# Retention attention on 64x64 quarter tiles of TensorE, and output written without transposes

## Chip, core and metric

The kernel runs on one core of a Trainium2 chip. The metric is the device time of one execution in microseconds (us). PE is the matrix engine TensorE, DVE, ACT and POOL are VectorE, ScalarE and GpSimdE, SP is the queue engine that issues all transfers here.

## What is computed

A decaying linear attention feeds two wide layers, all in float32 (the weights come as float64).

```python
B, H, S, D = 4, 8, 768, 64
gamma = 1.0 - 2.0 ** (-5.0 - np.arange(H))
for t in range(S):                       # state: B x H x D x D
    state = gamma * state + einsum('bhd,bhe->bhde', k[:, :, t], v[:, :, t])
    y[:, :, t] = einsum('bhd,bhde->bhe', q[:, :, t], state) / sqrt(D)
x = y.transpose(0, 2, 1, 3).reshape(3072, 512)
h = x @ w_in;  x = (h * cos(h)) @ w_out            # first layer, width 2048
h = x @ w_in2; x = elu(h) @ w_out2                 # second layer, width 2048
```

## The kernel before

The attention runs chunkwise. A unit is 128 tokens of one batch with all 8 heads; there are 24 units, four (one per batch) to a block of 512 tokens, six blocks. For unit n, chunk c = n // 4. `scores(n)` multiplies keys and queries (eight products, 64 deep, 128x128 out) and DVE masks the result into `pt`. `values(n)` adds, in PSUM, the state of the earlier chunks times the queries (for c > 0, eight products of 64x64 weights, 128 columns) and the values times `pt` (eight products, 128 deep, 64 wide, 128 columns). ACT and DVE split the sum into a high and a low part (`x_t`), the input of the first layer. `update(n)` multiplies keys and values of the unit into the state (eight products, 128 deep, 64x64). `state_unit(n)` makes the decayed state `aged(n)`; `scale_unit(n)` scales q and k.

The first layer's `hidden(blk, j)` takes block blk and the j-th of 8 pieces of the weights: 24 matmuls of 512 columns, then a chain of three ACT and two DVE passes out of PSUM. Attention of block blk + 1 stands between the `hidden` calls of block blk: `scores` before an even j, `values` after it, `update` after the next. During block 0 the weights are also decoded from float64 on ACT and DVE (`first_weights`), piece j being needed by `hidden(0, j)`.

Then come `project(0, ...)` (first layer out), `hidden2` and `project(1, ...)` (second layer). At the end each result tile `c`, which has features on the partitions and tokens along the free dimension, is turned by PE: `emit` makes two pieces of four 128x128 transposes each, with an ACT or DVE copy behind each piece, and writes rows of `out`; `last_half` does so for the two halves that are ready last. The list `turns` spreads these pieces between the matmul groups.

All instructions are recorded by `plan.op` with an engine, a supposed duration, and what they read and write. `Plan.deadlines` works out backward when each must begin. `Plan.run` then plays the program through on these durations and lets each engine take the ready instruction with the earliest deadline; PE keeps the recorded order. Operations of engine "ANY" go to DVE or POOL, whichever is free. Once the order is fixed, each engine's queue is strictly in order, SP's too. PSUM has three `eg` buffers of two banks (`hidden`, `scores`) and two `f` buffers of one bank (`values`, `update`, transposes).

Of the kernel before, what the change touches and what calls it, by code (L numbers as in the profile page):

```python
# [19 lines left out]
P = 128  # L20
# [4 lines left out]
TB = 512  # L25
# [6 lines left out]
WS = 4 * Q  # L32

# [41 lines left out]
class Plan:  # L75


    def __init__(self, slots):
        self.slots = slots
        self.ops = []  # L80
        self.queue = {tag: [] for tag in slots}

# [29 lines left out]
    def deadlines(self):  # L112
# [183 lines left out]
def retention_then_two_mlps(ctx: ExitStack, tc: tile.TileContext, attn, tab, weights, out):  # L296
# [22 lines left out]

    def dma(kb, out_, in_, r=(), w=(), lag=0):  # L320
        plan.op("SP", kb * PER_KB, lambda: nc.sync.dma_start(out=out_(), in_=in_()), r, w, lag)
# [120 lines left out]
    TAB, STATE, AGED, FALL = 0, 704, 1728, 2240  # L442
# [4 lines left out]
    def s_tab():  # L447
        return cst.t[:, 640:648].rearrange("p (h o) -> p h o", o=1)

    def g_tab():  # L450
        return cst.t[:, 648:652].rearrange("p (a o) -> p a o", o=1)
# [7 lines left out]

    def fall():  # L460
        return cst.t[:, FALL:FALL + H * P].rearrange("p (h t) -> p h t", h=H)
# [8 lines left out]
    fall_at = cst[FALL, FALL + H * P]  # L470
    unit, pt_t, x_t = {}, {}, {}
    tab_at = cst[TAB, TAB + 652]
# [8 lines left out]
    def scale_unit(n, lag=0):  # L481
# [5 lines left out]
        if n // B < UPB - 1:  # L487
            tt("ANY", (0.65, 1.25), k, k, lambda: s_tab().to_broadcast([P, H, D]), ALU.mult,
               [u[1536, 2048], tab_at], [u[1536, 2048]], lag=lag)
# [6 lines left out]

    def scores(n):
        u = unit[n]
        sc = Buf("eg", [P, 2, NPAIR, P])
        pt = Buf("w", [P, 2, NPAIR, P])  # L500
        pt_t[n] = pt

        def go():
# [8 lines left out]
        plan.op("PE", 1.0, go, [u[0, 1024]], [sc])  # L512
        flat = lambda x: (lambda: x.t.rearrange("p j a t -> p (j a) t"))
        tt("DVE", 1.23, flat(pt), flat(sc), fall, ALU.mult, [sc, fall_at], [pt], lag=-80)

    def values(n):
        c, b = divmod(n, B)
        u, pt = unit[n], pt_t.pop(n)


        xps = [Buf("f", [P, 2, P]) for _ in range(2)]

        def go():
            q = u.t[:, 0:512].rearrange("p (a t) -> p a t", a=NPAIR)
            for a in range(NPAIR if c > 0 else 0):
                for j in range(2):
                    r, o = slice(j * D, (j + 1) * D), j ^ (a % 2)
                    nc.tensor.matmul(  # L528
                        out=xps[a % 2].t[o * D:(o + 1) * D, a // 2, :], lhsT=aged(n)[r, a, :], rhs=q[r, a, :],
                        start=(a < 2), stop=False, skip_group_check=True,  # L530
                    )
            for a in range(NPAIR):
                for j in range(2):
                    h0, o = 1024 + (2 * a + j) * D, j ^ (a % 2)
                    nc.tensor.matmul(  # L535
                        out=xps[a % 2].t[o * D:(o + 1) * D, a // 2, :], lhsT=u.t[:, h0:h0 + D],
                        rhs=pt.t[:, j, a, :],
# [607 lines left out]
```

## Time and profile before

| what | us |
|---|---|
| median of three timed runs (1086.99 to 1088.24) | 1087.66 |
| profiled execution, first to last instruction (span) | 1086.3 |
| median less span: what lies around the span | 1.4 |
| PE busy in the span | 1063.6 |
| DVE busy | 807.5 |
| ACT busy | 659.9 |
| POOL busy | 229.1 |

Only the span of the profiled execution is recorded, not a time of its own beside it; the runs' median is set against it. An engine's busy time is the union of its instructions. Matmuls overlap in PE's pipeline, so a duration of one says little; the distance from one group's start to the next group's start is what it costs. A float32 matmul stands in the trace as two records. In the rows below, a timeline row has start, length, engine, line, what is written and read, tile and shape, and the number of records; brackets hold idle time before it and who ended it. A row of stretches has the stretch, its length, then each engine's busy time with its instructions, PE's granted clock (1.00 is 2.4 GHz), the share of the 16 transfer engines in use, and GB/s.

### The profile page before, as it was taken

Reading aid. Unit: us, or ns where it says so; the run is one execution under the profiler, and the core shown is the slowest. Engines: PE = TensorE matmul, PEld = TensorE weight load, DVE = VectorE, ACT = ScalarE, POOL = GpSimd, SP = SyncE. Lnnn points to the kernel's source line nnn. Section 1 sums busy time; section 2 is a strip of 40 time slices with the busy share of each in tenths; the row PEclk is TensorE's granted clock in tenths of the full one; section 3 lists DMA queues with packets and bytes.
Section 4 is the critical chain, followed back from the end, with each engine's and each line's share of the span. In section 5 each row is a group of like instructions: output and inputs, shape, how many; then the busy total and the mean of one; then the engine's idle time right before and its main releaser. Section 6 shows DMA issues by size and latency. Waiting matters only on the chain.

```text
span 1086.3 us, 15280 instructions
## 1 busy us (share of the span) xinstructions
PE 1063.6 (98%) x5704; PEld 856.5 (79%) x5704; DVE 807.5 (74%) x916; ACT 659.9 (61%) x805; POOL 229.1 (21%) x192
## 2 busy tenths in 40 slices
PE   7989999999999999999999999999999999999998
PEld 4767777778778888888887787777777888888886
DVE  6997787788789967657648898888889875565453
ACT  3876566655688753443445777877798744444442
POOL 3212550034114311000000453232223300010000
PEclk9999999999999999999999999999999999999999
DMA  9786999989999999999975558878868999999551
GB/s 345 298 281 215 338 325 324 329 277 350 328 323 336 317 326 335 337 342 329 348 293 195 221 229 303 311 293 323 314 232 280 361 349 298 385 326 326 200 204 59
DMA packets 115226, 323.32 MB, mean 298 GB/s; under 512 B 8656, under 2 KB 15440, under 8 KB 112592
## 3 DMA queue, kind: packets, MB, share of 16 engines
q1 hardware_dynamic: 115152, 322.35, 82.9%
q8 instruction: 45, 0.74, 0.3%
q14 instruction: 29, 0.24, 0.1%
HBM read 195.96 MB, written 126.35 MB: 297 GB/s over the span
## 4 chain that ended last, share of the span: by engine, by line
PE 84%; DVE 7%; ACT 4%; issue 2%; DMA 2%; POOL 0%; DVEq 0%; ACTq 0%; POOLq 0%
PE eg L907 41%; PE eg L607 23%; PE eg L680 11%; PE f L680 3%; ACT c L324 3%; PE eg L507 2%; PE f L535 2%; DVE c L329 2%; PE f L528 1%; DVE w L329 1%; DVE c L366 1%; PE f L808 1%; PE f L565 1%; DMA c<-in_weights 1%; ACT h L324 1%
## 5 line engine op out<-in xcount | busy, mean ns | idle before, releaser
L907 PE MATMUL eg<-hl,w 128*128 128x512 f32 x2016 | 464.2, 391 | 0.0
L907 PEld LDWEIGHTS eg<-hl,w 128*128 128x128 f32 x2016 | 376.7, 188 | 77.8 <-DVE h L837 0.3
L324 ACT ACTIVATE hl<-ld 128x1024 fp32r<-128x1024 f32 x168 | 177.5, 1060 | 232.8 <-PE eg L907 196.8
L329 DVE TENSOR_TENSOR hl<-ld,hl 128x1024 fp32r<-128x1024 f32 x168 | 209.8, 1260 | 106.5 <-ACT hl L324 106.3
L329 POOL TENSOR_TENSOR c<-c 128x512 f32<-128x512 f32 (+1 forms) x131 | 161.2, 1240 | 550.5 <-DVE c L329 126.7
L607 PE MATMUL eg<-hl,w 128*128 128x512 f32 x1152 | 274.8, 395 | 0.5 <-DVE w L329 0.5
L324 ACT ACTIVATE c<-c 128x1024 f32<-128x1024 f32 (+1 forms) x256 | 232.0, 919 | 40.7 <-DVE c L624 29.9
L607 PEld LDWEIGHTS eg<-hl,w 128*128 128x128 f32 x1152 | 213.9, 189 | 50.6 <-PE f L535 2.7
L324 ACT ACTIVATE c<-eg 128x1024 int32<-128x1024 f32 (+2 forms) x95 | 86.3, 908 | 73.2 <-PE eg L607 59.6
L329 DVE TENSOR_TENSOR c<-c 128x512 f32<-128x512 f32 (+2 forms) x137 | 91.5, 680 | 38.7 <-DMA c<-d 26.4
L680 PE MATMUL eg<-hl,w 128*128 128x512 f32 x432 | 111.3, 394 | 4.5 <-DVE c L329 1.9
L680 PEld LDWEIGHTS eg<-hl,w 128*128 128x128 f32 x432 | 79.9, 188 | 26.7 <-ACT h L324 3.8
L680 PE MATMUL eg<-ld,w 128*128 128x512 f32 x288 | 75.4, 399 | 2.2 <-ACT h L324 1.2
L629 DVE SCALAR_TENSOR_TENSOR c<-c,eg 128x1024 f32<-128x1024 f32 x48 | 58.4, 1218 | 19.5 <-ACT c L324 19.2
L624 DVE SCALAR_TENSOR_TENSOR c<-eg,c 128x1024 f32<-128x1024 f32 x48 | 58.6, 1221 | 13.9 <-ACT c L324 12.2
L680 PEld LDWEIGHTS eg<-ld,w 128*128 128x128 f32 x288 | 54.7, 192 | 16.4 <-ACT h L324 3.3
L329 POOL TENSOR_TENSOR ld<-ld,w 128x512 f32<-128x512 f32 x28 | 36.1, 1295 | 102.4 <-DMA ld<-in_attn 70.9
L423 DVE SCALAR_TENSOR_TENSOR w<-c,w 128x768 fp32r<-128x768 f32 (+1 forms) x48 | 56.7, 1196 | 1.3 <-ACT w L324 1.2
L366 DVE SCALAR_TENSOR_TENSOR c<-c,signs 128x512 uint32<-128x512 uint32 x64 | 51.2, 800 | 4.8 <-ACT signs L324 4.2
L324 ACT ACTIVATE signs<-c 128x512 f16<-128x512 f32 x64 | 50.1, 783 | 5.9 <-DVE c L366 4.7
L324 ACT ACTIVATE w<-c 128x1024 fp32r<-128x1024 f32 (+3 forms) x59 | 52.2, 916 | 0.3 <-PE eg L907 0.3
L324 ACT ACTIVATE h<-eg 128x512 f32<-128x512 f32 (+1 forms) x50 | 29.2, 584 | 34.8 <-PE eg L680 18.3
(62 smaller groups left out, 727.8 us busy)
## 6 DMA issues: line engine op xcount, KB each, us to landing
d<-c SPq DMA_DIRECT2D x205, 512.0 KB, 4.4
ld<-d SPq DMA_DIRECT2D x84, 1024.0 KB, 7.9
c<-d SPq DMA_DIRECT2D x93, 512.0 KB, 6.3
c<-in_weights SPq DMA_DIRECT2D x64, 512.0 KB, 6.1
ld<-in_attn SPq DMA_DIRECT2D x20, 1024.0 KB, 7.4
d<-h SPq DMA_DIRECT2D x32, 256.0 KB, 7.8
out<-c SPq DMA_DIRECT2D x11, 512.0 KB, 5.0
d<-c SPq DMA_DIRECT2D x16, 256.0 KB, 3.5
```

The costliest lines, as they stand in the source:

```text
L324: plan.op("ACT", us, lambda: nc.scalar.activation(out=out_(), in_=in_(), func=func, **kw), r, w, lag)
L329: return e.tensor_tensor(out=out_(), in0=a(), in1=b(), op=op)
L366: plan.op("DVE", 0.69, lambda: nc.vector.scalar_tensor_tensor(out=u(), in0=u(), scalar=3, in1=signs, op0=ALU.logical_shift_left, op1=ALU.b ...
L423: plan.op("DVE", 0.08 + 0.29 * (hi - lo), lambda: nc.vector.scalar_tensor_tensor(out=w.t[:, lo:hi, 1, :], in0=view(), scalar=turn, in1=hig ...
L507: nc.tensor.matmul(out=sc.t[:, j, a, :], lhsT=u.t[r, 512 + a * P:512 + (a + 1) * P], rhs=u.t[r, a * P:(a + 1) * P], start=True, stop=True,)
L528: nc.tensor.matmul(out=xps[a % 2].t[o * D:(o + 1) * D, a // 2, :], lhsT=aged(n)[r, a, :], rhs=q[r, a, :], start=(a < 2), stop=False, skip_ ...
L535: nc.tensor.matmul(out=xps[a % 2].t[o * D:(o + 1) * D, a // 2, :], lhsT=u.t[:, h0:h0 + D], rhs=pt.t[:, j, a, :], start=(c == 0 and a < 2), ...
L607: nc.tensor.matmul(out=h.t[:, half * TB:(half + 1) * TB], lhsT=quarter(j, qd, wpart, kc % 2), rhs=(xh, xl)[xpart].t[:, kc, :], start=(n == ...
L624: plan.op("DVE", 1.22, lambda: nc.vector.scalar_tensor_tensor(out=g.t, in0=h.t, scalar=1.0 / TWO_PI, in1=n(), op0=ALU.mult, op1=ALU.subtra ...
L629: plan.op("DVE", 1.22, lambda: nc.vector.scalar_tensor_tensor(out=g.t, in0=g.t, scalar=1.0, in1=h.t, op0=ALU.subtract, op1=ALU.mult,), [h, ...
L680: nc.tensor.matmul(out=out_(), lhsT=w.t[:, i, wpart, kc * P:(kc + 1) * P], rhs=x.t[:, xpart, kc, :], start=(start and n == 0), stop=(n == ...
L907: nc.tensor.matmul(out=acc.t[:, i * TB:(i + 1) * TB], lhsT=w[:, A_OF[p], wpart, i * P:(i + 1) * P], rhs=hl.t[:, gpart, k, :], start=(p in ...
```

## The change

Every product of the attention is cut into 64x64 tiles with 64 columns. A unit is now handled as two half chunks of 64 tokens.

- `scores(n)` holds the state products too (8 for each half chunk, into the same PSUM buffer) and 8 score products for each half chunk; for c = 0, 8 more between the halves. In the last chunk only the first half's state products are made. The mask pass covers 512 columns (768 for c = 0) where it covered 1024. `mid(n)`, the state between the halves, is a new DVE pass; for c = 0 DVE and not ACT stores the state. The keys of the last chunk are now scaled too.
- `carried(n)` (16 products with `aged` or `mid`) is a group of its own. A one-element POOL memset waits for it (`fence`), and `values(n)` (16 products, 24 for c = 0) waits for that memset.
- In blocks 1 to 4, `values(n)` and `scores(n + 1)` stand together before an even j, `carried(n + 1)` before the odd j. In block 0 they stand at tabulated places, some between the two halves of a `hidden`.
- The loads of the first four units and of weight pieces 0 and 1 get a fixed rank, so they go first and in that order.
- `emit` and `last_half` write `c` as it lies (4 KB or 2 KB a partition); transposes, their PSUM buffers and copies are gone, and the host permutes the result.

```diff
+        for n, rank in self.ranks.items():
+            start[n] = rank - 1e6
...
     def scores(n):
-        sc = Buf("eg", [P, 2, NPAIR, P])
-        pt = Buf("w", [P, 2, NPAIR, P])
+        c, batch = divmod(n, B)
+        blocks = [(ch, ch, ch * 2) for ch in range(2)] + ([(0, 1, 4)] if c == 0 else [])
+        wid = 2 * len(blocks) * HC
+        sc = Buf("eg", [P, 2, TB])
+        pt = Buf("w", [P, 2, wid])
+        sums = {0: (0, 0), 1: (0, 1)} if c else {0: (0, 0), 1: (0, 0)}
+        if c == UPB - 1:
+            del sums[1]
         def go():
-            for a in range(NPAIR):
-                for j in range(2):
-                    r = slice(j * D, (j + 1) * D)
-                    nc.tensor.matmul(
-                        out=sc.t[:, j, a, :], lhsT=u.t[r, 512 + a * P:512 + (a + 1) * P],
-                        rhs=u.t[r, a * P:(a + 1) * P], start=True, stop=True,
-                    )
-        tt("DVE", 1.23, flat(pt), flat(sc), fall, ALU.mult, [sc, fall_at], [pt], lag=-80)
+            for ch, (_, slot) in sums.items():
+                for a2 in range(2):
+                    for e in range(2):
+                        for j in range(2):
+                            h0, lo = at_head(j, ch, a2), wid + (slot * 2 + a2) * D
+                            r = slice(e * HC, (e + 1) * HC)
+                            nc.tensor.matmul(
+                                out=sc.t[j * D:(j + 1) * D, e, lo:lo + D],
+                                lhsT=u.t[r, 1536 + h0:1536 + h0 + D], rhs=u.t[r, 1024 + h0:1024 + h0 + D],
...
+            for cs, ct, at in blocks:
+                for a2 in range(2):
+                    for e in range(2):
+                        for j in range(2):
+                            r, h0 = slice(j * D, (j + 1) * D), (2 * a2 + e) * P
+                            ins = nc.tensor.matmul(
+                                out=sc.t[e * HC:(e + 1) * HC, j, (at + a2) * HC:(at + a2 + 1) * HC],
+                                lhsT=u.t[r, 512 + h0 + cs * HC:512 + h0 + cs * HC + HC],
+                                rhs=u.t[r, h0 + ct * HC:h0 + ct * HC + HC], start=True, stop=True,
...
+        plan.op("DVE", 0.42, lambda: after(nc.vector.tensor_tensor(
+            out=pair(mid(n)), in0=ds(0), in1=pair(aged(n)), op=ALU.add)), [sc, aged_at(n)], [mid_at(n)], -80)
...
+    def carried(n):
+            for ch, s in ((0, aged(n)), (1, mid(n))):
+                for a2 in range(2):
+                    for e in range(2):
+                        for j in range(2):
+                            r, o = slice(j * D, (j + 1) * D), j ^ e
+                            ins = nc.tensor.matmul(
+                                out=xps[e].t[o * D:(o + 1) * D, a2, ch * HC:(ch + 1) * HC], lhsT=s[r, e * 2 + a2, :],
+                                rhs=q[r, 2 * a2 + e, ch * HC:(ch + 1) * HC],
...
+        def fence():
+            ins = nc.gpsimd.memset(fences[0:1, n:n + 1], 0.0)
+            wait(ins, xps_t[n])
...
+        plan.op("POOL", 0.1, fence, xps, [fence_b[n]], -60)
...
+                            if n in xps_t:
+                                wait(ins, xps_t.pop(n))
...
-    def update(n):
...
-    def emit(sb, name, c, half, blk):
+    def emit(c, half, blk):
+        dma(4, lambda: out[blk, half], lambda: c.t, [c])
...
-                        nc.tensor.transpose(ps.t[:, k, :], c.t[:, lo + k * P:lo + k * P + P], ident)
+        dma(2, lambda: out[2 * sb, 1][:, i * TB:(i + 1) * TB], lambda: c.t, [c])
...
+    for k, n in ((0, 4), (3, 5), (7, 6), (11, 7), (14, 8)):
+        slots_of.setdefault((0, k), []).append((scores_of, n))
+    for k, n in ((2, 4), (6, 5), (10, 6), (13, 7), (15, 8)):
+        slots_of.setdefault((0, k), []).append((carried_of, n))
+    for k, n in ((3, 4), (7, 5), (11, 6), (14, 7)):
+        slots_of.setdefault((0, k), []).insert(0, (values_of, n))
+    for blk in range(1, NBLK - 1):
+        for i in range(B):
+            n = (blk + 1) * B + i
+            slots_of[blk, 4 * i] = [(values_of, n), (scores_of, n + 1)]
+            slots_of[blk, 4 * i + 2] = [(carried_of, n + 1)]
...
-    while turns:
-        turns.pop(0)()
```

On PE, in the middle of block 1, one unit's period stood so before (L607 is `hidden`, L565 `update`, L507 `scores`, L528 and L535 the two parts of `values`; a number behind x counts matmuls):

```order
L607 MATMUL eg<-hl,w 128x512 x24
L565 MATMUL f<-ld 64x64 x8
L507 MATMUL eg<-ld 128x128 x8
L607 MATMUL eg<-hl,w 128x512 x24
L528 MATMUL f<-ld,w 64x128 x8
L535 MATMUL f<-w,ld 64x128 x8
```

Of the change (L679 `hidden`, L598 `carried`, L629 `values`, L536 and L547 the state and score products of `scores`):

```order
L679 MATMUL eg<-hl,w 128x512 x24
L598 MATMUL f<-ld,w 64x64 x16
L679 MATMUL eg<-hl,w 128x512 x24
L629 MATMUL f<-w,ld 64x64 x16
L536 MATMUL eg<-ld 64x64 x16
L547 MATMUL eg<-ld 64x64 x16
```

There are still two breaks in the `hidden` stream per unit; 32 products became 64 smaller ones, and three groups of one tile size now adjoin.

On DVE, just before the first `hidden` of block 0, the rows before were these (`hl<-hl,w` scales unit 3, `hl<-f` makes the low part of the layer's input, `w<-c,w` the low part of weight piece 0, `w<-eg,w` is a mask):

```order
L329 TENSOR_TENSOR hl<-hl,w 128x512
L329 TENSOR_TENSOR hl<-f,hl 128x2x128
L329 TENSOR_TENSOR w<-c,w 128x4x256
L329 TENSOR_TENSOR hl<-f,hl 128x2x128
L329 TENSOR_TENSOR w<-eg,w 128x1024
```

Of the change (L563 is the mask, L572 the stored state, L374 a step of decoding weights, `ld<-ld,w` scales a unit):

```order
L563 TENSOR_TENSOR w<-eg,w 128x768
L572 COPY w<-eg 128x256
L374 SCALAR_TENSOR_TENSOR c<-c,signs 128x512
L337 TENSOR_TENSOR hl<-f,hl 128x2x128 x2
L337 TENSOR_TENSOR ld<-ld,w 128x512
L337 TENSOR_TENSOR w<-c,w 128x4x256
L337 TENSOR_TENSOR hl<-f,hl 128x2x128 x2
```

The last of these low parts, which the first `hidden` reads, had 24 DVE instructions ahead of it and has 33 now: two more scalings (fewer fall to POOL), four state copies, a copy for the mask table, a decoding step and a decayed state.

On SP, the first loads stood so before (`in_attn` are the units, `in_tab` tables, `in_weights` the float64 weights):

```order
L321 DMA ld<-in_attn 128x1024
L321 DMA w<-in_tab 128x652
L321 DMA ld<-in_attn 128x1024
L321 DMA ld<-in_attn 128x512 x2
L321 DMA ld<-in_attn 128x1024
L321 DMA ld<-in_attn 128x512 x2
L321 DMA c<-in_weights 128x1024
L321 DMA ld<-in_attn 128x512
L321 DMA c<-in_weights 128x1024
L321 DMA hl<-in_attn 128x1024
L321 DMA ld<-in_attn 128x512
L321 DMA ld<-in_attn 128x2048
```

Of the change:

```order
L327 DMA ld<-in_attn 128x1024
L327 DMA w<-in_tab 128x588
L327 DMA ld<-in_attn 128x512 x2
L327 DMA ld<-in_attn 128x1024
L327 DMA ld<-in_attn 128x512 x2
L327 DMA ld<-in_attn 128x1024
L327 DMA ld<-in_attn 128x512 x2
L327 DMA c<-in_weights 128x1024 x2
L327 DMA hl<-in_attn 128x1024
L327 DMA hl<-in_attn 128x512 x2
L327 DMA c<-in_weights 128x1024 x2
L327 DMA ld<-in_attn 128x2048
```

Each unit now comes whole before the next, and unit 4 (the last row of each) comes behind weight pieces 0 and 1.

## Rows read from the trace of the kernel before

**Rows 1.** The page's head and PE's busy time, share and instructions.
```profile
span 1086.3 us, 15280 instructions
PE 1063.6 (98%) x5704; PEld 856.5 (79%) x5704; DVE 807.5 (74%) x916; ACT 659.9 (61%) x805; POOL 229.1 (21%) x192
```

**Rows 2.** Stretches: opening, block 0, blocks 1 to 4, block 5, `project(1)`.
```profile
core 0: us, PE busy (x) PEld busy (x) DVE busy (x) ACT busy (x) POOL busy (x), PEclk, DMA share, GB/s
0.00:27.15 27.15, 21.13 (x232) 13.19 (x232) 17.76 (x25) 10.31 (x21) 8.95 (x11) 1.00 0.93 344
27.15:91.34 64.19, 61.06 (x450) 47.82 (x448) 58.60 (x74) 50.44 (x72) 14.74 (x13) 0.97 0.76 279
91.34:322.52 231.18, 231.18 (x1714) 183.43 (x1713) 185.51 (x231) 147.21 (x186) 67.36 (x58) 1.00 0.89 316
322.52:366.04 43.52, 43.52 (x193) 36.05 (x192) 39.60 (x44) 37.37 (x42) 15.67 (x20) 1.00 0.94 333
...
840.10:1086.30 246.20, 241.30 (x1105) 198.25 (x1103) 144.36 (x139) 110.66 (x118) 16.17 (x10) 1.00 0.80 280
```

**Rows 3.** Timeline of PE, one unit's period between blocks 1 and 3.
```profile
163.03 0.69 PE L565 MATMUL f<-ld 128*64 128x64 f32 x16
163.65 1.16 PE L507 MATMUL eg<-ld 64*128 64x128 f32 x16
164.74 5.76 PE L607 MATMUL eg<-hl,w 128*128 128x512 f32 x24
170.43 0.67 PE L528 MATMUL f<-ld,w 64*64 64x128 f32 x16
171.03 1.09 PE L535 MATMUL f<-w,ld 128*64 128x128 f32 x16
172.05 5.74 PE L607 MATMUL eg<-hl,w 128*128 128x512 f32 x24
177.72 0.69 PE L565 MATMUL f<-ld 128*64 128x64 f32 x16
```

**Rows 4.** Timeline of PE matmuls begun before 47.63 us.
```profile
47.61 0.34 PE L528 MATMUL f<-ld,w 64*64 64x128 f32 x4
```

**Rows 5.** Timeline of PE weight loads begun before 47.69 us.
```profile
47.61 0.21 PEld L528 LDWEIGHTS f<-ld,w 64*64 64x64 f32 x8 [0.35 <-issue]
```

**Rows 6.** Stretches of block 0, DVE busy alone, then clock and transfers.
```profile
27.15:42.00 14.85, 14.33 (x17) 1.00 0.90 352
42.00:57.00 15.00, 14.66 (x19) 1.00 0.72 253
57.00:72.00 15.00, 14.53 (x20) 0.89 0.77 268
```

**Rows 7.** Timeline of PE around its longest wait in block 0.
```profile
65.75 0.98 PE L528 MATMUL f<-ld,w 64*64 64x128 f32 x16 [2.61 <-DVE hl L329]
```

**Rows 8.** Groups of DVE and POOL in blocks 1 to 4, shapes apart.
```profile
L329 DVE TENSOR_TENSOR w<-eg,w 128x1024 f32<-128x1024 f32 x16 | 19.5, 1217 | 3.3 <-PE eg L507 3.1
L329 DVE TENSOR_TENSOR c<-c 128x512 f32<-128x512 f32 x27 | 18.7, 692 | 0.7 <-POOL c L329 0.2
L329 DVE TENSOR_TENSOR w<-f,w 128x256 f32<-128x256 f32 x12 | 5.0, 421 | 12.4 <-PE f L565 12.4
L329 POOL TENSOR_TENSOR c<-c 128x256 f32<-128x256 f32 x3 | 2.2, 740 | 24.1 <-DMA d<-c 20.8 <-DVE c L329 2.3 <-DVE c L366 1.1
```

**Rows 9.** Timeline of PE, `project(1)` up to its first transposes.
```profile
840.08 46.41 PE L907 MATMUL eg<-hl,w 128*128 128x512 f32 x204
886.33 0.60 PE L808 MATMUL f<-ident,c 128*128 128x128 f32 x4
```

**Rows 10.** Timeline of all engines, the end.
```profile
1080.68 0.39 PE L907 MATMUL eg<-hl,w 128*128 128x512 f32 x1
1081.52 0.42 DVE L837 COPY h<-eg 128x256 f32<-128x256 f32 x1 [2.74 <-ACT h L324]
1082.97 0.37 SPq L321 DMA_DIRECT2D out<-h  x1
```

More of the change, by code (lines that the diff above doesn't have):

```diff
@@ new lines, in go, with after, mask @@
+            last.append(ins)
+            return ins
+        plan.op("PE", 1.05 if c else 1.2, go, [u], [sc])
+        def after(ins):
+            wait(ins, last[0])
+            return ins
+        def mask():
+            return after(nc.vector.tensor_tensor(
+                out=pt.t.rearrange("p j (h t) -> p j h t", t=HC),
+                in0=sc.t[:, :, 0:wid].rearrange("p j (h t) -> p j h t", t=HC),
+                in1=fall()[:, :, 0:wid // HC, :], op=ALU.mult))
+        plan.op("DVE", 0.68 if c else 0.95, mask, [sc, fall_at], [pt], -80)
@@ new lines, in scores, with go @@
+        if c < UPB - 1:
+            plan.op("DVE", 0.42, lambda: after(nc.vector.tensor_tensor(
+                out=pair(state(batch)), in0=ds(1), in1=pair(mid(n)), op=ALU.add)),
+                [sc, mid_at(n)], [state_at(batch)], -40)
+    xps_of, xps_t, fence_b = {}, {}, {}
+    fences = keep.tile([1, NU], F32, name="fences")
+    def carried(n):
+        u = unit[n]
+        xps = [Buf("f", [P, 2, P]) for _ in range(2)]
+        xps_of[n] = xps
+        def go():
+            q = u.t[:, 0:512].rearrange("p (a t) -> p a t", a=NPAIR)
+            for ch, s in ((0, aged(n)), (1, mid(n))):
[6 more added lines that the diff above has]
+                                rhs=q[r, 2 * a2 + e, ch * HC:(ch + 1) * HC],
+                                start=(ch == 0 and a2 == 0), stop=False, skip_group_check=True,
+                            )
+            xps_t[n] = ins
+        plan.op("PE", 0.6, go, [u[0, 512], mid_at(n), aged_at(n)], xps)
+        fence_b[n] = Buf(None, [1, 1])
+        fence_b[n].t = fences
+        def fence():
+            ins = nc.gpsimd.memset(fences[0:1, n:n + 1], 0.0)
+            wait(ins, xps_t[n])
+            xps_t[n] = ins
+            return ins
+        plan.op("POOL", 0.1, fence, xps, [fence_b[n]], -60)
@@ L516, in values @@
     def values(n):
         c, b = divmod(n, B)
-        u, pt = unit[n], pt_t.pop(n)
-        xps = [Buf("f", [P, 2, P]) for _ in range(2)]
+        u, pt = unit.pop(n), pt_t.pop(n)
+        xps = xps_of.pop(n) if c else [Buf("f", [P, 2, P]) for _ in range(2)]
+        blocks = [(ch, ch, ch * 2) for ch in range(2)] + ([(0, 1, 4)] if c == 0 else [])
         def go():
[L524 to L537, printed above, removed]
-                        start=(c == 0 and a < 2), stop=(a >= NPAIR - 2), skip_group_check=True,
-                    )
@@ L543, in values @@
+        plan.op("PE", 0.6 if c else 0.8, go, [u[1024, 1536], pt] + ([fence_b[n]] if c else []), xps)
         if b == 0:
@@ L617, in hidden @@
             plan.op("PE", 12 * MM, go, [xh, xl] + need, [h[half * TB, half * TB + TB]])
+            if half == 0:
+                for step, n in between:
+                    step(n)
         u = Buf("c", [P, 2 * TB])
```

256 lines of the change are left out of this document (111 added, 145 removed).

## Prediction

> **What bounds the kernel now.** I began with the page's head: PE is busy for 98% of a span of 1086.3 us [rows 1]. A share alone does not say that work taken from PE shortens the run, so I split the span at stage boundaries [rows 2]. In blocks 1 to 4 PE is busy for all of 231.18 us, in block 5 for all of 43.52 us. There PE's own work is the time, and the other engines have room (DVE 185.51 of 231.18). Block 0 is different: 64.19 us, of which PE works 61.06, with a granted clock of 0.97. Then I looked at one unit's period on PE [rows 3], at how quickly products on different tiles start [rows 4, 5], at DVE in block 0 [rows 6, 7], at single costs on DVE and POOL [rows 8], and at the end of the program [rows 9, 10].
>
> Block 5 holds no attention, so it gives the price of `hidden` alone: 43.52 us for 192 matmuls, 0.2267 each, 5.44 for the 24 of one call [rows 2]. Four blocks of that are 174.1, so attention costs blocks 1 to 4 the other 57.1 us. [Rows 3] split this by the distance between starts: `update` 163.03 to 163.65, 0.62; `scores` to 164.74, 1.09; the state part of `values` 170.43 to 171.03, 0.60; its other part to 172.05, 1.02; together 3.33 us a unit. A `hidden` between them takes 5.69 and 5.67 where it takes 5.44 undisturbed, so each break in its stream costs 0.24 more.
>
> **Attention on quarter tiles.** First the price of the new groups. `update` is 8 passes of 64 columns on two tiles at a time, 0.62; `scores` is 8 passes of 128 columns on two tiles, 1.09 [rows 3]. The difference, 0.47, is what 8 times 64 columns cost, so a pass of 64 columns is 0.059 us, and 0.15 of a group is its beginning and end. The open question is whether four 64x64 tiles run together at this pace. The nearest row is the state part of `values`, which uses 64x64 tiles: its 16 records of 128 columns take 0.60, the 16 records on two half-wide tiles behind it take 1.02 [rows 3]. Four of its matmuls begin within 0.03 us [rows 4], and eight weight loads begin within 0.09 us, so that loads do not queue for each other beyond one round [rows 5]. I take four abreast. Bounds for a group of 16 new products (8 passes of four tiles): 0.62 if all four run together as the two do in `update`, 1.09 if two at a time (16 passes of 0.059 and 0.15).
>
> So `carried` costs 0.62. `values` and `scores` together are 24 passes: 1.56 as one run (0.15 and 24 times 0.059), 1.71 if the beginning and end are paid twice. The rows show no boundary between two groups of the same tile size, so both ends stay; I take 1.60, nearer to one run, because within a group the next tile follows without a gap. (The Trainium skill, TensorEngine Tiling (Array Packing), Key Properties, says that a change of tiling mode drains TensorE and a change of tile alone does not. By it the boundary would be free, 1.56; [rows 3] show only boundaries with a change of mode, so they neither support nor deny it.)
>
> A unit then costs 2.22 where it cost 3.33, with the same two breaks. In the last chunk the pair has 20 passes, 1.32 to 1.47, I take 1.36. From the first `hidden` of block 1 to the end of block 4, PE did 12 `update`, 15 `scores` and 16 `values`: 7.4, 16.4 and 25.9, in all 49.7 us. Of the change it does 11 full pairs (17.6), 4 short ones (5.4), 15 `carried` (9.3) and one lone `values` (0.6): 32.9. Breaks are 31 in both. **Saved: 16.8 us** (14.7 with every boundary paid, 17.4 with none). One `carried` and one set of state products have moved into block 0.
>
> What else must keep up there? DVE's mask falls from 1.22 us to about 0.69, while `mid` adds 0.42 [rows 8], so DVE has no more work than before, 185.5 us in 214. The PSUM of a `hidden` is reused two calls later: the time in between falls from about 9 us to 8 us, against 5.4 us for which it is left alone in block 5's stream twice over (10.9). Transfers are the tighter side: 0.89 of the engines over 231 us becomes 0.96 over 214, and the highest share that the rows show without a PE wait is 0.94 [rows 2]. I put **1 us back** for that, 0 to 5.
>
> **Opening and block 0.** DVE is busy for 43.5 of the first 44.9 us of block 0 [rows 6], and PE's longest wait there, 2.61 us, ends with DVE [rows 7]. Saving PE's time in this stretch mostly makes PE wait longer. DVE's work is about equal: four masks less half, four `mid` more. Before the first `hidden` it grows: two scalings and a decoding step at 0.69, four state copies and a decayed state at 0.42, less four shorter masks (0.27 each, estimated between the rows for 512 and 1024 columns) and a mask table that is 0.1 cheaper; 2.1 + 2.1 - 1.1 - 0.1, near 3 us. Against it stand 9.4 us in which DVE is idle in the opening (17.76 busy of 27.15 [rows 2]); loads in the order of need should fill some of this. I let the first `hidden` come 1.5 us later (1 earlier to 3 later). After 72 us DVE has room (the other 15.1 of its 58.6 us in 19.3 [rows 2, 6]), and the last `hidden` calls of block 0 stand with cheaper groups: about 2.5 us back, with part of the wait's consequences. **Net 1 us less** until block 1, from 4 less to 4 more.
>
> The fixed order of the loads alone moves no bytes: the units were first before too, and it is the tables that DVE waits for, whose place is unchanged. I cost it at nothing beyond the above; it is hidden behind DVE, and if DVE were faster it would be worth less than the 1.5 us.
>
> The fence puts POOL between `carried` and `values`. The wait is covered by a `hidden` of 5.44 us; POOL is busy for 67 of 231 us [rows 2]. Cost: nothing, unless a POOL instruction ahead of the memset itself waits (below).
>
> **Output.** From its first matmul at 840.08 to the last at 1080.68 plus 0.23, `project(1)` takes 240.8 us on PE [rows 9, 10]. Its 1008 matmuls at 0.2267 (204 of them take 46.25 [rows 9]) are 228.5. The rest, 12.3, is transposes, the breaks beside them and the waits of the last halves. All of it goes: **12.3 us**. The copies behind the transposes are not on the path. At the end, the halves are copied by 1081.94, then turned and copied again, and the last transfer is issued at 1082.97 [rows 10]; now it can be issued at 1082.0: **0.95 us**. Its own time I leave as it is.
>
> **Sum.** Of the span of 1086.3: -1.0 - 16.8 + 1.0 - 12.3 - 0.95 = -30.05, so 1056.2; with the 1.4 us that lie around it, 1057.6 us. The median stands to the span as before (1087.66 to 1086.3).
>
> **Rivals.**
> *Two tiles at a time.* If 64x64 tiles with 64 columns run in pairs, a pass of four costs 0.117 us. Then a pair of groups costs 2.96 and `carried` 1.09, 4.05 a unit where it was 3.33. Blocks 1 to 4: 60 in place of 49.7, 10.3 more; block 0 and the opening 4 to 5 more by the same price; output 13.3 less: 1088 to 1091, not faster, and slower from about 0.11 us a pass on. Against it: [rows 4], four starts within 0.03 us, though with 128 columns. Chance 0.05.
>
> *A floor for each matmul.* If starts kept a distance of 0.025 us whatever the tile, four would need 0.10 us, hidden in today's passes of 128 columns but not in those of 64. Pairs 2.55, short pairs 2.15, `carried` 0.95: 52 in place of 49.7; with the output about 1077. Against it: [rows 4] again, whose four starts would fill 0.075 us and not 0.03. Chance 0.03. (The Trainium skill, TensorE: Matmul & The Clock Gate, Part 1, gives about 25 ns as the least distance of starts however small the matmul; by that rule this rival would win. The trace disagrees for matmuls on different tiles, by the 0.03 us.)
>
> *Someone else becomes the bound in blocks 1 to 4.* Transfers, at a share of 0.89 already, or a fence late behind a POOL instruction that waits for its own transfer: one such wait was 20.8 us [rows 8], and a `values` would wait for what exceeds 5.4 us. Before, PE waited for neither there. If half of the 16.8 is lost, 1066; if all, 1074. Chance 0.13.
>
> *Less than forecast*, if the opening improves too and boundaries are free: under 1052, chance 0.04.
>
> **The numbers.** The forecast has 0.75, with its own range of 1052 to 1063. Its bounds add up to: -4, -17.4, 0, -12.3, -1, which gives 1053, and +4, -14.7, +5, -12, -0.9, which gives 1069. The range 1052 to 1067 leaves out the first two rivals, the worse half of the third and the last. Faster by over 0.2% (what a measurement of this kernel can just tell from no change, 2 us) holds for all but the first rival: 0.94; same 0.02; slower 0.04.
>
> **What would show it.** `carried` near 0.62 from start to start, `values` and `scores` together near 1.6, an unbroken `project(1)` of 228.5 us, blocks 1 to 4 near 215 with PE busy throughout, first `hidden` between 26 and 30 us. Passes of 0.1 us and more, PE waits on POOL or on transfers in blocks 1 to 4, or a block 0 over 68 us would prove me wrong.

## The result, and the profile after

The changed kernel takes **1059.6 us** (median of four runs, 1058.5 to 1060.6), the kernel before in runs beside it 1088.0: ratio 0.973, 95% interval 0.971 to 0.975. The profiled execution took 1058.54, its span is 1056.8, where [rows 1] had 1086.3. The forecast was 1057.6, its span 1056.2. The total is close; its parts are not all. The median lies 2.0 above the forecast: 0.6 in the span, 0.3 because 1.7 us and not 1.4 lie around it, and 1.1 because the execution that was profiled was the fastest of the four. For the same reason the spans differ by 29.5 where the medians differ by 28.3.

The page of the changed kernel, head, PE's busy row and the queues that bring instructions:

```profile
span 1056.8 us, 18290 instructions
PE 1028.8 (97%) x7204; PEld 832.6 (79%) x7208; DVE 806.6 (76%) x931; ACT 651.5 (62%) x788; POOL 230.8 (22%) x213
...
q8 instruction: 56, 0.92, 0.4%
q14 instruction: 29, 0.24, 0.1%
```

PE has 34.8 us less to do than in [rows 1] and is idle for 28.0 us where it was idle for 22.7. So about 5 us of PE's saving came back as waiting. The stretches say where (opening, block 0, blocks 1 to 4, `hidden2`, `project(1)` to the end; to be held against [rows 2]):

```profile
core 0: us, PE busy (x) PEld busy (x) DVE busy (x) ACT busy (x) POOL busy (x), PEclk, DMA share, GB/s
0.00:30.98 30.98, 20.31 (x596) 13.19 (x600) 18.98 (x32) 10.67 (x20) 6.53 (x9) 0.93 0.93 339
30.98:95.67 64.69, 61.09 (x836) 46.89 (x832) 59.33 (x82) 49.10 (x69) 14.93 (x19) 0.95 0.74 267
95.67:308.16 212.49, 212.02 (x2568) 170.83 (x2561) 180.56 (x250) 141.69 (x180) 61.32 (x63) 1.00 0.93 331
...
580.16:822.51 242.35, 234.09 (x1009) 187.52 (x1008) 211.20 (x259) 195.35 (x264) 89.22 (x73) 1.00 0.79 284
822.51:1056.80 234.29, 229.28 (x1009) 188.85 (x1007) 137.20 (x128) 103.97 (x104) 12.51 (x9) 1.00 0.82 289
```

One correction makes the first three comparable. The new group of `values` and `scores` that ends block 0 does 1.5 us of work (94.12 to 95.67) where before `update` and `scores` stood, and block 0 also holds a `carried` more. (The prediction says "from the first `hidden` of block 1", but its count of 11 full pairs includes this one; from 95.67 on there are 10. So its sum has to be held against the time from 94.12.) Measured from the point at which that group begins, 94.12, opening and block 0 together are 2.8 us longer than the 91.34 of before, and blocks 1 to 4 take 214.04 (to 308.16), 17.1 less than 231.18. `hidden2` took 245.55 before (below) and is 3.2 shorter, `project(1)` to its last matmul 10.7 shorter (240.6 to 229.9), and from there to the end it is 1.2 shorter. Block 5 and `project(0)` are unchanged to 0.1. The sum: +2.8 - 17.1 - 3.2 - 10.7 - 1.2 = -29.4, the difference of the spans within rounding.

The timeline of PE in the middle of block 1 shows the price of a unit; it answers to [rows 3]:

```profile
155.96 0.69 PE L598 MATMUL f<-ld,w 64*64 64x64 f32 x32
156.58 5.74 PE L679 MATMUL eg<-hl,w 128*128 128x512 f32 x24
162.25 0.69 PE L629 MATMUL f<-w,ld 64*64 64x64 f32 x32
162.76 0.65 PE L536 MATMUL eg<-ld 64*64 64x64 f32 x32
163.23 0.65 PE L547 MATMUL eg<-ld 64*64 64x64 f32 x32
163.81 2.56 PE L679 MATMUL eg<-hl,w 128*128 128x512 f32 x10
```

`carried` costs 0.62 (155.96 to 156.58), `values` with `scores` 1.56 (162.25 to 163.81), in all 2.18 where it was 3.33. The three groups follow each other at 0.51 and 0.47, and the middle one's 0.47 is just eight passes of 0.059: the joint between groups of one tile size is free.

The opening is where the forecast failed. PE there, from the `values` of the second unit to the first `hidden` (L679; L629 is `values`, L536 and L547 `scores`, L996 filler matmuls):

```profile
17.49 0.80 PE L629 MATMUL f<-w,ld 64*64 64x64 f32 x39
21.77 0.35 PE L629 MATMUL f<-w,ld 64*64 64x64 f32 x9 [3.47 <-issue]
21.94 0.68 PE L536 MATMUL eg<-hl 64*64 64x64 f32 x32
22.41 0.91 PE L547 MATMUL eg<-hl 64*64 64x64 f32 x48
23.25 0.82 PE L996 MATMUL eg<-c 128*128 128x512 bf16 x2
24.00 0.79 PE L629 MATMUL f<-w,ld 64*64 64x64 f32 x35
26.09 0.45 PE L629 MATMUL f<-w,ld 64*64 64x64 f32 x13 [1.29 <-issue]
27.93 1.24 PE L629 MATMUL f<-w,hl 64*64 64x64 f32 x48 [1.38 <-DVE hl L337]
29.55 0.69 PE L536 MATMUL eg<-ld 64*64 64x64 f32 x32 [0.38 <-DVE ld L337]
30.07 0.99 PE L547 MATMUL eg<-ld 64*64 64x64 f32 x32
30.98 0.79 PE L679 MATMUL eg<-hl,w 128*128 128x512 f32 x1
```

Twice PE stops in the middle of a group of 48 records, after 39 and after 35, with nothing that it waits for ("issue"), for 3.47 and 1.29 us. Nothing differs there in the operands. A third such stop, of 0.48 us, cuts the first `hidden` itself: its first record begins at 30.98, the second at 32.10 after a wait of 0.33 for DVE, and only from 33.80 on does it run unbroken. From 30.19 to 37.01 PE's granted clock is 0.50, that is 1.2 GHz, after waits of 1.29, 1.38 and 0.38 us, and from 9.71 to 13.12 too, after one of 1.98; in the opening of the kernel before it stays at 1.00 [rows 2]. So this `hidden` gives way to the next group only at 40.30, 9.3 us after its first record; in the kernel before that took 5.7 (27.15 to 32.82). And DVE in the stretch of the first stop:

```profile
18.44 0.69 DVE L337 TENSOR_TENSOR hl<-hl,w 128x512 f32<-128x512 f32 x1
22.57 0.76 DVE L337 TENSOR_TENSOR hl<-f,hl 128x256 fp32r<-128x256 f32 x2 [3.44 <-ACT hl L332]
```

DVE's next row in its queue is the low part of the very `values` group in which PE stopped, so DVE stands idle for 3.44 us too. Before, DVE had no gap of over 0.2 us between 17.2 and 28.5 us.

### The profile page after: what moved, and what is told of

Same layout as the page of the kernel before. It is cut to its first block, busy times and chain, and to the rows that moved or that the text cites. A ratio compares the mean times of both kernels' runs of the same rounds, so it can differ in the third digit from the quotient of the medians.

```text
span 1056.8 us, 18290 instructions
## 1 busy us (share of the span) xinstructions
PE 1028.8 (97%) x7204; PEld 832.6 (79%) x7208; DVE 806.6 (76%) x931; ACT 651.5 (62%) x788; POOL 230.8 (22%) x213
## 5 line engine op out<-in xcount | busy, mean ns | idle before, releaser
L679 PE MATMUL eg<-hl,w 128*128 128x512 f32 x1152 | 277.0, 397 | 3.0 <-DVE c L704 1.5
L337 POOL TENSOR_TENSOR c<-c 128x512 f32<-128x512 f32 (+1 forms) x141 | 173.3, 1240 | 479.5 <-DVE c L337 170.4
L679 PEld LDWEIGHTS eg<-hl,w 128*128 128x128 f32 x1152 | 214.2, 189 | 51.5 <-DVE w L337 1.9
L699 DVE SCALAR_TENSOR_TENSOR c<-eg,c 128x1024 f32<-128x1024 f32 x48 | 58.6, 1220 | 19.2 <-ACT c L332 17.1
L377 DVE SCALAR_TENSOR_TENSOR c<-c 128x512 uint32<-128x512 uint32 x64 | 52.6, 831 | 0.7
L374 DVE SCALAR_TENSOR_TENSOR c<-c,signs 128x512 uint32<-128x512 uint32 x64 | 50.2, 785 | 0.8 <-ACT signs L332 0.5
L332 ACT ACTIVATE h<-eg 128x512 f32<-128x512 f32 (+1 forms) x50 | 29.2, 584 | 29.1 <-PE eg L755 10.7
```

The lines of the kernel that those rows point to most:

```text
L332: plan.op("ACT", us, lambda: nc.scalar.activation(out=out_(), in_=in_(), func=func, **kw), r, w, lag)
L337: return e.tensor_tensor(out=out_(), in0=a(), in1=b(), op=op)
L374: plan.op("DVE", 0.69, lambda: nc.vector.scalar_tensor_tensor(out=u(), in0=u(), scalar=3, in1=signs, op0=ALU.logical_shift_left, op1=ALU.b ...
L377: plan.op("DVE", 0.69, lambda: nc.vector.scalar_tensor_tensor(out=u(), in0=raw.t[:, :, 0], scalar=29, in1=u(), op0=ALU.logical_shift_right ...
L679: nc.tensor.matmul(out=h.t[:, half * TB:(half + 1) * TB], lhsT=quarter(j, qd, wpart, kc % 2), rhs=(xh, xl)[xpart].t[:, kc, :], start=(n == ...
L699: plan.op("DVE", 1.22, lambda: nc.vector.scalar_tensor_tensor(out=g.t, in0=h.t, scalar=1.0 / TWO_PI, in1=n(), op0=ALU.mult, op1=ALU.subtra ...
```

## What the experiments asked

My theory after this reading: the long group of quarter tiles is as cheap as forecast because four tiles run together, and the opening is late because PE runs out of instructions. Between the two breaks above lie 9 + 32 + 48 + 2 + 35 = 126 matmul records, with a weight load for each 252 instructions. The page's queue q8 brought 45 packets in the kernel before, 56 now, while PE's records (PE and PEld) rose from 11408 to 14412: 254 and 257 of them to a packet. The kernels below fit as well (e1 11216 in 44, e2 14608 in 57, e7 13773 in 54). So q8 carries PE's program in pieces of about 255 records, 16 KB each (0.92 MB in 56), and the breaks lie one piece apart.

The kept traces hold the times of these packets, and they settle this part. In the changed kernel three packets have landed at 20.38, 24.78 and 32.33, and PE goes on at 21.77, 26.09 and 33.80: 1.39, 1.31 and 1.47 later. Seven of the traces have such stops, 18 in all. Each ends 1.2 to 1.5 us after a packet of q8 has landed, and each lies right behind the 222nd, 349th, 476th or 603rd weight load of the program (127 apart; in e6, whose opening has other groups, behind the 221st). What they cost is the open question, and the experiments ask it. The rivals for the late opening: it comes from the work that was put ahead of the first `hidden` on DVE and PE; or from the order of the loads.

### Each half of the change alone (e1, e2)

e1 takes the attention of the kernel before with the new `emit` and `last_half`; e2 takes the new attention with the old `emit` and `last_half` (the diff above, one part each).

> The kernel before with the new output alone (no transposes, tiles of the result written as they lie), attention as before. Theory: the output part is worth 10.7 us of PE in the last stage plus 1.2 us at the end, as the two profiles differ there, and touches nothing else: span about 1074.4, time about 1076. Rival: part of what the whole change gained in the second layer's first half (3.2 us less there than before) comes from it: then about 1073.

> The changed kernel with the old transposed output. Theory: blocks 1 to 4 gain 17 us, the opening loses about 3, and the second layer's first half gains 3 by the order that the planner now finds, not by the output: about 1071. Rival: that 3 us belongs to the output part or to chance: about 1074.

Measured: e1 **1074.07** (ratio 0.987, 0.985 to 0.989), e2 **1073.25** (0.987, 0.984 to 0.989). Of 1088.2 they save 14.1 and 14.9; both together saved 28.3. Within the noise the halves add up and don't help or harm each other. In e1 `project(1)` to its last matmul takes 229.5, 11.1 less than before, and its tail 4.4 (5.6 before). In e2 the opening lasts 32.4 and blocks 1 to 4 take 212.9, so both the loss and the gain belong to the attention. Each time lies between the two that were expected.

### The loads without their fixed order (e3)

```diff
-            plan.ranks[n] = opening[0] + len(plan.ranks) * 1e-3
+            pass
```

> The changed kernel with the loads of the opening ordered by the planner again. Theory: PE's pauses inside a group of products in the opening (3.5 and 1.3 us, no semaphore shown) come from PE running out of instructions: it now takes some 1000 of them before the first hidden call where it took 400, fetched in pieces of 16 KB; the load order does not matter, so the first hidden call stays at 30 to 32 us and the time within 2 us of the changed kernel. Rival: the fixed order fills the transfer engines early and so holds the fetches back; without it the pauses shrink and the first hidden call comes near 27 us, 3 to 6 us less in all.

Measured **1062.98** (0.978, 0.974 to 0.982), first `hidden` at 36.4, later than with the order: both expectations missed. PE's waits in e3 up to the first `hidden` (what waited for whom: total, times, longest):

```profile
PE eg L536 <- DMA ld<-in_attn: 3.7, 1, 3.7
PE eg L536 <- DMA hl<-in_attn: 3.2, 1, 3.2
PE f L629 <- issue: 3.0, 3, 1.3
```

The changed kernel has 0.3 us of transfers there. So the fixed order is not hidden behind DVE: it brings each unit whole before PE needs it. How late the opening then is can't be read from this one trace: e3's profiled execution was the longest of its runs, with PE at half clock from 23.8 to 37.4 us and again for 6.8 us in `project(0)`. The medians say 3.4 us, and the intervals just meet.

### More instructions in the opening, and fewer (e4, e6)

e4 cuts twelve of the filler matmuls into four pieces each, 36 more matmuls with their loads for about the same columns. e6 merges, for the first four units, the products of the first half's keys or values with both halves of queries into one product of 128 columns: 16 products less in `scores` and `values` together for each unit.

```diff
-            for _ in range(n):
-                nc.tensor.matmul(out=rest_ps.t, lhsT=rest.t[:, 0:P], rhs=rest.t, start=True, stop=True)
+            for _ in range(n * cut):
+                nc.tensor.matmul(out=rest_ps.t[:, 0:TB // cut], lhsT=rest.t[:, 0:P], rhs=rest.t[:, 0:TB // cut],
+                                 start=True, stop=True)
...
-    warm(3)
+    warm(3, 4)
```

and e6, in `scores` and `values` alike:

```diff
-            for cs, ct, at in blocks:
+            for cs, ct, at in blocks[:2]:
+                wide = c == 0 and cs == 0
...
+                            rhs = u.t[r, q0:q0 + (P if wide else HC)]
```

> The changed kernel, but each of the four groups of three idle matmuls of 512 columns that stand between the first units is cut into twelve of 128 columns (they compute nothing that is used): the same columns, 72 more PE instructions in the opening. Theory (PE runs out of instructions): pauses without a semaphore grow, the first hidden call comes 1 to 3 us later than in the changed kernel (30.98). Rival (loads, or a wait that the profile doesn't show): the first hidden call moves by less than 0.5 us.

> The changed kernel, but in the first chunk the score products of the early keys with both halves of the queries, and the products of the early values with both, are one product of 128 columns each instead of two of 64: 48 instead of 64 products for each of the first four units, same columns. Theory (PE runs out of instructions in the opening): 256 PE instructions fewer, one piece of 16 KB, so one of the pauses goes: first hidden call 2 to 4 us earlier than 30.98, 0 to 3 us less in all since the vector engine holds block 0. Rival: columns or loads set the opening, nothing moves by more than 0.5 us.

Measured: e4 1060.59 (0.975, 0.972 to 0.977) with the first `hidden` at 34.81, 3.8 later; e6 **1057.12** (0.970, 0.967 to 0.973) with it at 30.19, 0.8 earlier. The theory's direction holds both ways; by this mark e4 moved more than expected and e6 less. (The interval of e6's time still touches the changed kernel's, 0.971 to 0.975.) PE in e4:

```profile
16.31 0.52 PE L629 MATMUL f<-w,ld 64*64 64x64 f32 x20 [1.39 <-issue]
...
22.25 0.82 PE L629 MATMUL f<-w,ld 64*64 64x64 f32 x35 [3.04 <-issue]
...
33.66 0.36 PE L536 MATMUL eg<-ld 64*64 64x64 f32 x1 [2.55 <-issue]
```

7.0 us of "issue" before the first `hidden` where the changed kernel had 4.8, at other places of the groups; a stretch at half clock from 22.8 to 26.2 us adds to the 3.8 as well, so it is not the pauses alone. e6 has one such stop left, of 2.13 us, so one piece less did take one stop away.

The start of the first record is a poor mark, though, since in the changed kernel that `hidden` stands still twice behind it. By the group that follows the first `hidden`, e4 is 2.5 us later than the changed kernel (42.82 for 40.30) and e6 3.2 earlier (37.13), and so both lie in the ranges that were expected of the first `hidden`. The time of the whole moved by 1.0 and by 2.5.

### The order of tiles (e5)

```diff
-                for a2 in range(2):
-                    for e in range(2):
+                for e in range(2):
+                    for a2 in range(2):
```

> The changed kernel with the two innermost loops but one exchanged, so that consecutive products of the attention use only two of the four tiles in turn, then the other two. Same products, same instructions. Theory (four tiles run together): taken two at a time a pass of 64 columns costs 0.059 us for two tiles, so a group of 16 goes from 0.62 to about 1.09 us, a unit's groups from 2.18 to about 4.06; over 15 units in blocks 1 to 4 some 28 us, about 35 us in all: near 1094. Rival (the order of tiles does not matter, the columns or the instructions set the pace): within 3 us of 1060.

One run: 1064.27, 4.7 us over the changed kernel's median, where 35 were expected: the theory on the order fell. (The rival's 3 us were passed too, by a single run.) PE's timeline in e5, at the joint of `values` and `scores`:

```profile
150.97 0.68 PE L629 MATMUL f<-w,ld 64*64 64x64 f32 x30
151.49 0.22 PE L536 MATMUL eg<-ld 64*64 64x64 f32 x1
151.49 0.22 PE L629 MATMUL f<-w,ld 64*64 64x64 f32 x1
151.50 0.22 PE L536 MATMUL eg<-ld 64*64 64x64 f32 x1
```

Products of `scores` begin before the last ones of `values`, which stand ahead of them in the queue. So between tiles PE's queue does not start strictly in order: here PE starts a later product on an idle tile, and an order by pairs costs only 0.05 us a group (`carried` 158.33 to 159.00 in this trace, 0.67 for 0.62). That left open whether four tiles run together at all, and e9 was made for it.

### Two tiles only (e9)

```diff
-                            r, o = slice(j * D, (j + 1) * D), j ^ e
+                            r, o = slice(j * D, (j + 1) * D), j
```

> The changed kernel, but the 16 products of carried write to the partitions that they read from, so they use two of the four tiles; the number, size and order of products are the same. The output is changed: in half of the heads the earlier chunks' part lands in the neighbouring head. Theory (four tiles run together, and two tiles would cost 16 passes of 0.059 us and 0.15 at the ends): carried takes 1.09 us from start to start where it took 0.62, about 0.47 longer, 20 times in all, of which 15 in blocks 1 to 4; that stretch becomes about 7 us longer (219 to 220 us where the changed kernel had 212.5), the whole 7 to 9 us longer, near 1067. Rival (tiles run at most in pairs, or the pace is set by something else such as the issue of instructions): carried stays within 0.1 us of 0.62, the time within 3 us of 1060.

One run: 1065.06, span 1063.3, and on PE:

```profile
157.64 1.15 PE L598 MATMUL f<-ld,w 64*64 64x64 f32 x32
158.72 5.74 PE L679 MATMUL eg<-hl,w 128*128 128x512 f32 x24
```

`carried` takes 1.08 from start to start, with the same 16 products, and blocks 1 to 4 take 219.1, 6.6 longer. The theory named 1.09 and 219 to 220. Four quarter tiles do run abreast, at the pace that two have, and two at a time would have cost what the first rival charged for it.

### First four units in whole chunks (e7, e8), and unit 4 later (e10)

e7 handles only the first four units as the kernel before did (eight products of 128 columns, own `update0`, mask of 1024 columns), the rest as changed; e8 is e7 without the fixed order of the loads; e10 is e7 with `scores(4)` moved behind the first half of the first `hidden`.

```diff
-    scores(0)
+    scores0(0)
...
-        scores(n)
+        values0(n - 1)
+        scores0(n)
...
-        values(n - 1)
+        update0(n - 1)
```

and for e10 besides:

```diff
-    for k, n in ((0, 4), (3, 5), (7, 6), (11, 7), (14, 8)):
+    for k, n in ((1, 4), (3, 5), (7, 6), (11, 7), (14, 8)):
```

> The first chunk's four units as in the kernel before (whole chunks of 128 tokens, 24 products of 128 or 64 columns each, their keys and values packed for it, an own mask), everything else as in the changed kernel. Theory: PE needs some 400 instructions before the first hidden call and not some 1000, so no pause without a semaphore; first hidden call at 25 to 28 us, no half clock at the start of block 0; block 0 is held by the vector engine, so only 2 to 5 us of it remain at the end: 1055 to 1057. Rival (the late opening came from the order of the vector engine's work): first hidden call within 1.5 us of 30.98.

> As the kernel with whole first chunks, but with the planner's order of the first loads. Theory: with PE's instructions no longer short, the fixed order is worth little: within 2 us of that kernel. Rival: the order by need is worth the 3 us that it was worth in the changed kernel, whatever PE's instructions do.

> The version with whole chunks for the first four units (e7), with scores of unit 4 moved from ahead of the first hidden call to between its two halves; nothing else. This takes one scaling pass (0.69 us) of unit 4 out of DVE's queue ahead of the low part that the first hidden waits for, and 16 quarter products out of PE's queue there. Theory (DVE's order holds the first hidden): it begins 0.6 to 1.5 us earlier than in e7 (29.97), at 28.5 to 29.4, and the whole is 0 to 2 us under e7 (1055.5), since block 0 has to do the moved work. Rival (something else holds it, PE's instruction supply or a transfer): the first hidden begins within 0.4 us of 29.97 and the whole within 1 us of e7.

Measured: e7 **1055.52** (0.968, 0.966 to 0.971), the first `hidden` at 29.97; e8 **1053.92** (0.968, 0.965 to 0.971), at 31.0; e10 **1056.13** (0.970, 0.968 to 0.973), at 27.85. e7 and e8 are the best versions, 4 to 6 us under the changed kernel; all their runs (1052.7 to 1057.4) lie below all of its own (1058.5 to 1060.6). For e7 the time came out as the theory said and the place as the rival said: the stops inside groups are gone, but the first `hidden` begins only 1.0 earlier, and most of the rest came in block 0 (61.1 for 64.7). Of these 3.6 us 2.5 lie in the first `hidden` call (29.97 to 36.81, 6.8 us for 9.3): it has no stop in it, and half clock for 2.5 us of it where the changed kernel has 6.0. With few products in the opening the fixed order is worth nothing that can be measured (e8 against e7, whose runs overlap).

In e10 the order of the work holds the first `hidden`. DVE and then PE, e10:

```profile
26.11 0.69 DVE L337 TENSOR_TENSOR ld<-ld,w 128x512 f32<-128x512 f32 x1
26.71 0.75 DVE L337 TENSOR_TENSOR hl<-f,hl 128x256 fp32r<-128x256 f32 x2
```

```profile
27.23 0.69 PE L722 MATMUL f<-hl 128*64 128x64 f32 x16 [1.43 <-issue]
27.85 3.02 PE L764 MATMUL eg<-hl,w 128*128 128x512 f32 x12
30.79 0.69 PE L538 MATMUL eg<-ld 64*64 64x64 f32 x32
```

and PE of e7 at the same place:

```profile
27.88 0.69 PE L722 MATMUL f<-hl 128*64 128x64 f32 x16 [2.04 <-issue]
28.50 0.69 PE L538 MATMUL eg<-ld 64*64 64x64 f32 x32
29.01 1.02 PE L549 MATMUL eg<-ld 64*64 64x64 f32 x32
29.97 2.50 PE L764 MATMUL eg<-hl,w 128*128 128x512 f32 x5
```

One scaling less ahead on DVE let `update0` (L722) go 0.65 earlier; the other 1.47 are the products of `scores(4)` themselves, which no longer stand ahead of the `hidden`. But block 0 takes 2.3 longer in e10 (63.4 for 61.1) and the total is the same: the 2.1 us were given back at once. So the place moved as the theory said, and further, and the time stayed within the rival's 1 us. The "issue" of 2.04 in e7 is by all signs a wait, for the `f` buffer that the first of DVE's two low parts frees at 27.78 (e10: free at 27.13, PE at 27.23):

```profile
27.36 0.75 DVE L337 TENSOR_TENSOR hl<-f,hl 128x256 fp32r<-128x256 f32 x2
```

The label covers what the profile can't name. A stop in the middle of a group, at a place that goes by the count of instructions and that ends behind a packet of q8, is what tells the program's supply apart.

### The openings side by side

Each row is one execution. e1 has the opening of the kernel before, e2 and e9 have that of the changed kernel, so these rows also show how far two executions of one opening lie apart: up to 1.5 us. Differences of that size (0.8 and 1.0 in the first `hidden` of e6 and e7, 0.65 in `update0` of e10) are not shown to come from what was changed. The last but one column is where the group begins that begins at 94.12 in the changed kernel (in the first two rows: the first `hidden` of block 1).

| kernel | stops inside groups ahead of the first `hidden` | first `hidden` begins | group behind it begins | block 0 done | median |
|---|---|---|---|---|---|
| before | none | 27.15 | 32.82 | 91.34 | 1088.0 |
| e1 | none | 26.23 | 31.90 | 90.10 | 1074.1 |
| changed | 4.8 | 30.98 | 40.30 | 94.12 | 1059.6 |
| e2 | 4.2 | 32.43 | 39.21 | 92.96 | 1073.3 |
| e9 | 3.0 | 31.37 | 38.80 | 94.52 | 1065.1 |
| e4 | 7.0 | 34.81 | 42.82 | 95.87 | 1060.6 |
| e6 | 2.1 | 30.19 | 37.13 | 91.19 | 1057.1 |
| e7 | none | 29.97 | 36.81 | 89.54 | 1055.5 |
| e10 (`scores(4)` inside the first `hidden`) | none | 27.85 | 34.83 | 89.65 | 1056.1 |

By the last columns a late opening is not cheap: from the changed kernel to e7 3.5 us at the first `hidden`'s end became 4.6 at the end of block 0 and 4.1 in the whole, and to e6 3.2 became 2.9 and 2.5. Of e4's 2.5 later 1.8 were left at the end of block 0 and 1.0 in the whole. Only from e7 to e10 is the gain given back whole (2.0 became nothing).

## Why the prediction was right, and where it was not

**Attention in blocks 1 to 4: right.** Forecast 16.8 saved with 1.0 put back, measured 17.1 saved over the same groups (from 94.12). `carried` is 0.62 as taken; the pair is 1.56, the lower bound, where 1.60 was taken. (The Trainium skill, TensorEngine Tiling (Array Packing), Key Properties, says that a change of tile alone does not drain TensorE; the trace agrees, 0.51 and 0.47 between the three starts.) The 1 us put back for transfers was not needed: at a share of 0.93 PE waited 0.5 us in that stretch, and for DVE. The fence cost nothing; no wait of PE there ends with POOL.

**The rivals on four tiles: refuted.** A pass of four is 0.059, and e9 shows what a pass of two would have made of it. (The Trainium skill, TensorE: Matmul & The Clock Gate, Part 1, gives about 25 ns as the least distance of starts. As an estimate by it, the 32 records of a group would need 0.80 us; the trace disagrees across tiles, 0.47 for 32 records in a run of groups, 0.015 each.) The rival of another engine as the bound did not come up: PE's waits from 94.12 to 308.16 are the 0.5 us.

**Opening and block 0: wrong in sign.** Forecast 1.0 less, measured 2.8 more. The step that failed is "I let the first `hidden` come 1.5 us later": it came 3.8 later, outside the 3 that were allowed, and its call was done 7.5 later (40.30 for 32.82). What the forecast left out is the count of PE's instructions: the opening now needs 596 matmul records where it had 232 [rows 2], and when they are used up faster than the program arrives, PE stops, and DVE, next in its own queue for PE's result, stops with it (3.44 us). It also had no term for a lower clock, which the first `hidden` then had for 6.0 of its 9.3 us. The stops are shown to be the program's supply by the packets of q8; their number and sum go with the count of instructions (7.0 in e4, 3.0 to 4.8 in the changed opening, 2.1 in e6, none in e7). e10 shows that the order of the work holds the first `hidden` as well. Of the 7.5, whole units in the opening took away 3.5 (e7, with no stop and less half clock), and one group moved out of the way 2.0 more (e10); the last 2.0 are not accounted for, nor how the 3.5 divide between stops and clock. With whole units the term comes out close to its forecast: block 0 is done at 89.5 and 89.7 in e7 and e10, 1.8 and 1.7 before the 91.34.

The other half of the term, block 0 itself, was right in kind: from the first `hidden` to 94.12 it takes 63.1, 1.0 less than 64.19 (2.5 were forecast), though its first `hidden` call takes 9.3 for 5.7; the rest is 4.7 shorter. In that rest PE's waits end with DVE (all but 0.2 us). DVE is as busy as in [rows 6]:

```profile
46.00:61.00 15.00, 13.76 (x177) 10.99 (x176) 14.16 (x20) 10.98 (x16) 2.97 (x4) 1.00 0.76 265
61.00:76.00 15.00, 13.72 (x176) 10.38 (x176) 14.75 (x20) 13.04 (x20) 3.45 (x4) 1.00 0.69 258
```

14.16 and 14.75 of 15 us. That fits the gain of e10, given back wholly; the gains of e6 and e7 were kept.

**The fixed order of the loads: "at nothing" was wrong** for this kernel. Without it two transfers end PE's longest waits (e3), and by the medians the time is 3.4 us longer, with intervals that just meet. "Nothing" holds only where the opening has few products (e8).

**Output: right in kind, 1.6 too much.** 12.3 forecast, 10.7 measured. The term held that the waits of the last halves would go; one stays. PE near the end waits for the copy that frees its PSUM buffer:

```profile
1047.48 0.38 ACT L332 ACTIVATE h<-eg 128x256 f32<-128x256 f32 x1 [5.74 <-PE eg L925]
1047.90 0.42 DVE L877 COPY h<-eg 128x256 f32<-128x256 f32 x1 [4.86 <-ACT h L332]
...
1048.38 4.38 PE L925 MATMUL eg<-hl,w 128*128 128x512 f32 x18 [0.93 <-DVE h L877]
```

That is 0.93 of the 1.6. **The end**: 0.95 forecast, 1.2 measured.

**`hidden2`: not in the sum, and 3.2 shorter.** The stretch of the kernel before, in the columns of [rows 2]:

```profile
594.55:840.10 245.55, 236.91 (x1010) 188.51 (x1009) 210.47 (x261) 195.27 (x264) 86.39 (x69) 0.99 0.76 278
```

PE's waits are the same in both (8.6 idle before, 8.3 after), but its busy time is 2.8 less. The kernel before had 3.4 us at half clock there, which is 1.7; the changed one none. e1, with the old attention and no half clock there, takes 244.0, 1.5 less. The rest, about 1.7, comes with the new attention: the kernels that have it take 241.2 (e2), 242.4 (changed), 241.7 (e9) and 241.3 (e7). Nothing in this stage itself was changed, and what in the planner's order brings it is open. Without this stage's 3.2 the span would have been 1060.0, so the 3.8 lost in the opening term and the 3.2 won here cancel: that the sum came nearer than its parts was luck.

## What to carry to other kernels

Cutting a product into quarter tiles pays on PE exactly as passes count, where PE is the bound and the instructions flow; at the start of a program, count PE's instructions as well as its columns, and keep products whole there. Mark a stage by where its work runs unbroken, not by its first record: from the changed kernel to e6 the first `hidden` begins 0.8 earlier, its call is done 3.2 earlier, and the whole is 2.5 shorter. And compare two executions of one kernel before a difference of 1 us in one trace is read as an effect. An order of loads is worth what waits for them, so it has to be tried again when the work behind it changes.

## What the runs showed that was not expected

PE's program arrives in pieces of about 255 records of matmuls and weight loads (45 packets for 11408, 56 for 14412). Where 596 records fell into the first 31 us, PE stood still for up to 3.5 us at the end of a piece, and went on 1.2 to 1.5 us after the next one had landed. Whether the busy transfers (a share of 0.93, before and after) delay the pieces is not shown. In blocks 1 to 4, where a unit's 128 quarter records alternate with `hidden`, no such stop is seen. PE starts later products on idle tiles ahead of earlier ones that wait for their tile (e5), so the order of tiles inside a group is worth only 0.05 us of 0.62. And the label "issue" hides waits for a PSUM buffer as well as for instructions; the place of the stop and the packets of the instruction queue tell them apart.
